# Chunked attention with a feed-forward: row-paired scores, a second batch by DMA transposes, a reordered front

## The chip, the cores and the metric

One NeuronCore of a Trainium2 chip. The metric is device time of one execution in microseconds (us); the kernel before takes 217.55 us (median of 3 runs, 217.46 to 218.55). Each profile is of one execution, and its span (first to last instruction) is some 1.7 us shorter than its time: 216.0 us for the kernel before. Times of different jobs differ a little (they ran on different chips), so every kernel below was timed in alternation with the kernel before, and the ratio of the two is what is compared.

## The reference, cut to what matters

```python
# 4 batches, 8 heads, 768 rows, head size 64, 8 memory rows; chunks of 32 rows,
# each sees 16 rows to the left, itself, 8 rows to the right and the memory
for c in range(S // 32):
    k_full = concat(mem_k, k[l_start:r_end]);  v_full = concat(mem_v, v[l_start:r_end])
    a = softmax(q[c] @ k_full.T / sqrt(64))
    out[c] = a @ v_full
x  = heads side by side                      # 4 x 768 x 512
xn = (x - mean) / sqrt(var + 1e-6) * g_ln
y  = x + max(xn @ w_ch1, 0) @ w_ch2          # 512 -> 2048 -> 512
```

The 3072 rows are 24 tiles of 128 rows; three tiles make a unit, two units a batch. Units and batches are counted from 0 here: what the recorded texts call the second unit is unit 1. "Up" and "down" are the two projections of a unit. The attention of a unit's three tiles runs among the projections of the unit before it.

## The kernel before: the parts that matter

Everything is scheduled by hand. A unit's program has 28 numbered steps: 16 column groups of the up projection, then 12 pieces of the down projection. `at(step, f)` puts other work into a step.

Scores take two heads at once on all 128 rows of TensorE. For this the queries lie in a buffer that is half zeros, `QZ`:

```python
def scores(b, t):                       # before
    for gg in range(2):
        for j in range(4):              # pair of heads
            nc.tensor.matmul(out=p[:, gg, 128 * j : 128 * j + 128],
                lhsT=KT[...128 rows, 128 columns], rhs=QZ[b % 2][:, g, j, :, :])   # 128 columns, half zeros
```

Keys and queries must be turned (head size onto the partitions). Batches 0 and 1 are turned on TensorE from a few large loads (four for batch 1, rows of 1 KB); batches 2 and 3 come as twelve token loads each (128 KB in rows of 128 B) and are turned by DMA transposes issued on SyncE ("crossbar"):

```python
def load_tokens(b, which, t): nc.gpsimd.dma_start(...)            # 128 tokens x 8 heads x 128 B
def cross_k(b, half, t0, t1): nc.sync.dma_start_transpose(KT, kraw)
def k_around(b, t0, t1):      4 x nc.gpsimd.tensor_copy(KT, KT)   # borders: a chunk's neighbours
def load_v_head(b, h):        nc.gpsimd.dma_start(V, v)           # values, batches 2 and 3
def v_around(b):              2 x nc.sync.dma_start(V, V)         # value borders
... cut ...
if u == 0: ... load_kq x4, load_v_group x6 for batch 1, inverse roots of tiles 0-2 at steps 19 to 21
if u == 1: kq_block(1, j, ...) at 5 and 11        # batch 1 turned on TensorE
           load_tokens(2, ...) x12 at 14
if u == 2: cross(2) at 0, 1; k_around at 8; load_v_head x8 at 8; second half of cross(2) at 14, 15
if u == 3: v_mem(2), v_around(2) at 1; k_around at 4
```

GpSimd issues the loads, SyncE the transposes, the output stores and the border copies; each works through its queue in order. GpSimd also computes each tile's inverse root, 1/sqrt(var + 1e-6), in that order.

The softmax here doesn't subtract the row's maximum and nothing guards it: scores larger than these inputs give would overflow.

## Time and profile before

| | kernel before |
|---|---|
| time, median (range) | 217.55 us (217.46 to 218.55) |
| span of the profile | 216.0 us |
| TensorE busy | 97% of the span |
| first up matmul (unit 0) | 18.27 us |
| unit 1 starts | 47.37 us |
| unit 2 starts | 74.65 us |
| unit 3 starts | 98.06 us |
| unit 4 starts | 121.39 us |

The unit starts are the starts of the first up matmul of each unit in the matmul timeline. In the line below the fields are packets, bytes, mean rate and how many packets were small:

```profile
DMA packets 87714, 27.37 MB, mean 127 GB/s; under 512 B 78297, under 2 KB 84185, under 8 KB 87642
```

### The profile page before, as it was taken

Reading aid. Unit: us, or ns where it says so; the run is one execution under the profiler, and the core shown is the slowest. Engines: PE = TensorE matmul, PEld = TensorE weight load, DVE = VectorE, ACT = ScalarE, POOL = GpSimd, SP = SyncE. Lnnn points to the kernel's source line nnn. Section 1 sums busy time; section 2 is a strip of 40 time slices with the busy share of each in tenths; the row PEclk is TensorE's granted clock in tenths of the full one; section 3 lists DMA queues with packets and bytes.
Section 4 is the critical chain, followed back from the end, with each engine's and each line's share of the span. In section 5 each row is a group of like instructions: output and inputs, shape, how many; then the busy total and the mean of one; then the engine's idle time right before and its main releaser. Section 6 shows DMA issues by size and latency. Waiting matters only on the chain.

```text
span 216.0 us, 5059 instructions
## 1 busy us (share of the span) xinstructions
PE 210.2 (97%) x2011; PEld 129.8 (60%) x2011; DVE 118.6 (55%) x274; ACT 99.7 (46%) x206; POOL 104.4 (48%) x185
## 2 busy tenths in 40 slices
PE   7999989999999999999999999999999999999993
PEld 2557866557765577546754676456754675466562
DVE  6967675685737548524375349224484447634222
ACT  4478437855893677302653167103761275314100
POOL 7993245699996318974004998507145000400000
PEclk9999999999999999999999999999999999999998
DMA  5999999999999989996312999997674101330012
GB/s 78 182 150 207 209 208 181 200 206 226 148 140 172 102 135 146 151 146 171 48 27 80 142 186 148 138 156 103 176 150 132 49 3 24 91 108 0 0 49 100
DMA packets 87714, 27.37 MB, mean 127 GB/s; under 512 B 78297, under 2 KB 84185, under 8 KB 87642
## 3 DMA queue, kind: packets, MB, share of 16 engines
q0 software_dynamic: 62128, 14.38, 78.2%
q1 hardware_dynamic: 25562, 12.66, 28.2%
q8 instruction: 16, 0.26, 0.5%
q14 instruction: 8, 0.07, 0.1%
HBM read 28.84 MB, written 6.29 MB: 163 GB/s over the span
## 4 chain that ended last, share of the span: by engine, by line
PE 94%; DVE 3%; ACT 1%; issue 1%; ACTq 0%
PE mm L377 37%; PE mm L394 37%; PE att L289 5%; PE att L309 3%; PE mm L366 3%; PE att L179 2%; PE mm L412 2%; PE mm L179 1%; DVE QZ L436 1%; ACT AT L296 1%; PE att L352 1%; PE att L366 1%; DVE rT L385 1%; PE mm L539 0%; DVE xn L329 0%
## 5 line engine op out<-in xcount | busy, mean ns | idle before, releaser
L377 PE MATMUL mm<-xT,w1c 128*128 128x384 f16 (+2 forms) x560 | 89.0, 313 | 0.6 <-DVE rT L385 0.6
L394 PE MATMUL mm<-w2c,rT 128*128 128x512 f16 x368 | 84.4, 379 | 0.0
L377 PEld LDWEIGHTS <-w1c 128*128 128x128 f16 x560 | 58.8, 114 | 23.6 <-issue 1.0
L383 ACT ACTIVATE rT<-mm 128x384 f16<-128x384 f32 (+2 forms) x74 | 33.1, 453 | 72.4 <-PE mm L377 50.2
L394 PEld LDWEIGHTS <-rT 128*128 128x128 f16 x368 | 34.7, 98 | 37.5
L385 DVE TENSOR_SCALAR rT<-mm 128x384 f16<-128x384 f32 (+2 forms) x66 | 34.9, 533 | 33.6 <-PE mm L377 33.5
L401 DVE SCALAR_TENSOR_TENSOR osb<-mm,rstd,xs 128x512 f32<-128x512 f32 x23 | 17.3, 750 | 41.8 <-PE mm L394 24.9
L296 ACT ACTIVATE AT<-att,band 104x512 f16<-104x512 f32 x48 | 30.2, 683 | 9.6 <-PE att L289 8.2
L338 POOL TENSOR_SCALAR veps<-squares 128x1 f32<-128x1 f32 x24 | 4.8, 200 | 42.7 <-ACT junk L335 41.3
L117 POOL DMA_DIRECT2D V<-in_v_dram x24 | 18.4, 772 | 11.0 <-DMA w1c<-in_moe_w_ch_dram 7.8
L335 ACT ACTIVATE junk<-xs,nmean 128x512 f16<-128x512 f32 x24 | 17.3, 721 | 7.1 <-DVE nmean L326 6.7
L329 DVE SCALAR_TENSOR_TENSOR xn<-xs,nmean,g_row 128x512 f16<-128x512 f32 x24 | 18.8, 782 | 0.9
L320 DVE SCALAR_TENSOR_TENSOR xs<-att,rec 128x512 f32<-128x512 f32 x24 | 16.6, 691 | 0.8
L289 PEld LDWEIGHTS <-KT 128*128 128x128 f16 x192 | 12.6, 98 | 4.6 <-issue 1.0
L277 POOL COPY QZ<-kraw 64x768 f16<-64x768 f16 x16 | 13.2, 826 | 3.9 <-DMA kraw<-qraw 3.4
L342 POOL TENSOR_TENSOR rstd<-veps,mhalf 128x1 f32<-128x1 f32 x24 | 13.7, 571 | 2.0
L289 PE MATMUL att<-QZ,KT 128*128 128x128 f16 x192 | 14.6, 219 | 0.0
L269 POOL COPY KT<-KT 128x128 f16<-128x128 f16 (+4 forms) x16 | 4.2, 292 | 18.2 <-DMA KT<-kraw 18.1
L123 POOL DMA_DIRECT2D V<-in_v_dram x16 | 12.0, 791 | 0.9 <-PE mm L377 0.7
L309 PEld LDWEIGHTS <-AT 104*64 104x64 f16 x384 | 7.5, 111 | 6.5 <-ACT AT L296 2.1
L242 POOL DMA_DIRECT2D qraw<-in_q_dram x12 | 11.3, 938 | 0.0
L242 POOL DMA_DIRECT2D kraw<-in_k_dram x12 | 11.2, 934 | 0.0
(76 smaller groups left out, 136.6 us busy)
## 6 DMA issues: line engine op xcount, KB each, us to landing
out_dram<-osb SPq DMA_DIRECT2D x23, 256.0 KB, 2.3
V<-in_v_dram POOLq DMA_DIRECT2D x36, 96.0 KB, 6.9
w1c<-in_moe_w_ch_dram POOLq DMA_DIRECT2D x4, 512.0 KB, 9.6
w2c<-in_moe_w_ch_dram POOLq DMA_DIRECT2D x4, 512.0 KB, 13.5
kraw<-in_k_dram POOLq DMA_DIRECT2D x12, 128.0 KB, 5.3
qraw<-in_q_dram POOLq DMA_DIRECT2D x12, 128.0 KB, 5.4
qraw<-in_q_dram POOLq DMA_DIRECT2D x3, 384.0 KB, 11.6
kraw<-in_k_dram POOLq DMA_DIRECT2D x3, 256.0 KB, 5.7
```

The lines of the kernel that those rows point to most:

```text
L117: nc.gpsimd.dma_start(out=V[b % 2][r : r + hi - lo, g, :, 0:64], in_=dram(v, b * H * HS + lo * D, [[64, hi - lo], [HS, H], [1, 64]]),)
L242: nc.gpsimd.dma_start(out=free(dst, 512 * t, [[64, H], [1, 64]]), in_=dram(src, b * H * HS + 128 * t * D, [[D, 128], [HS, H], [1, 64]]),)
L289: nc.tensor.matmul(out=p[:, gg, 128 * j : 128 * j + 128], lhsT=KT[b % 2][:, (4 * g + j) * KW : (4 * g + j) * KW + 128], rhs=QZ[b % 2][:, g ...
L296: nc.scalar.activation(out=free(a, 32 * c, [[512, 2], [64, 8], [1, 32]], KR), in_=free(p, 32 * c, [[512, 2], [64, 8], [1, 32]], KR), func= ...
L320: nc.vector.scalar_tensor_tensor(out=x.rearrange("p (h d) -> p h d", h=H), in0=free(p, 0, [[128, H], [1, 64]]), scalar=1.0, in1=free(r, 0, ...
L329: nc.vector.scalar_tensor_tensor(out=xn[i], in0=x, scalar=nmean[i], in1=g_row, op0=ALU.add, op1=ALU.mult,)
L335: nc.scalar.activation(out=junk, in_=xs[xi], func=ACTF.Square, bias=nmean[i], accum_out=squares[i],)
L377: nc.tensor.matmul(out=p, lhsT=free(w, i, [[4, 128]]), rhs=xT[u % 2][:, dt, lo:hi], start=(dt == 0), stop=(dt == 3),)
L383: nc.scalar.activation(out=o, in_=p, func=ACTF.Relu)
L385: nc.vector.tensor_scalar(out=o, in0=p, scalar1=0.0, scalar2=None, op0=ALU.max)
L394: nc.tensor.matmul(out=p, lhsT=rT[hc][:, 128 * i : 128 * i + 128], rhs=w2c[hc // 4][:, hc % 4, :], start=(hc == 0), stop=(hc == 15),)
L401: nc.vector.scalar_tensor_tensor(out=o, in0=p, scalar=rstd[t % 9], in1=xs[t % 9], op0=ALU.mult, op1=ALU.add,)
```

## The change

Its intent: scores of two heads run side by side, each on 64 of TensorE's rows, with dense queries, so that half of the streamed columns and all copies that spread queries into a zeroed buffer go; batch 1 is turned by the crossbar as batches 2 and 3 are, which takes 128 transposes off TensorE; and the front is reordered so that the first tile's work comes first, with batch 0's memory values copied on VectorE rather than by DMA.

```diff
-            nc.tensor.matmul(out=p[:, gg, 128*j : ...], lhsT=KT[b % 2][:, ...128],
-                             rhs=QZ[b % 2][:, g, j, :, :])
+            for par in range(2):
+                rows = slice(64 * par, 64 * par + 64)
+                nc.tensor.matmul(out=p[:, par, 64*(4*gg+j) : ...+64], lhsT=KT[b % 2][rows, ...128],
+                                 rhs=QT[b % 2][rows, ...64], tile_position=(64 * par, 0))
... cut: spread_q, clear_q and QZ go; keep_q copies once instead of twice ...
 # the front
-    v_mem(0)                               # memory rows of V by DMA
-    for g in range(6): load_v_group(0, g)
+    for g in range(3): load_v_group(0, g)  # the other three behind the band's arithmetic
+    keep_mem(0, 0, 6, vec)                 # memory rows of V on VectorE
+    # g_row: two one-row FP32 matmuls between the first and the second transposes
 ... cut: other filler counts between the pieces (stay_busy) ...
-    for hc in range(3): up(0, 1, hc, 0, True)     # first tile alone
+    for hc in range(2): up(0, 2, hc)              # two tiles
 # unit 0
-            for h in (0, 4):
-                for which in range(2): at(15, load_kq, 1, which, 0, 96, h, h + 4)
-            for g in range(6): at(23, load_v_group, 1, g)
+            for t in range(6):
+                for which in range(2): at(15, load_tokens, 1, which, t)
 # unit 1
-            kq_block(1, ...) at 5 and 11;  load_v_group(1, 6..11) at 0
+            cross(1) at 0 to 3;  k_around(1, 0, 4) at 8;  load_v_group(1, 0..1) at 8
+            k_around(1, 4, 6) at 13;  load_v_group(1, 2..11) at 13
 # units 2 and 3, for batch 2
-            cross(2) at 0, 1 and 14, 15;  k_around and load_v_head x8 at 8
+            cross(2) at 14, 15 and 17, 18;  k_around and load_v_head x8 at 22
-            v_mem, v_around at 1;  k_around at 4        (unit 3)
+            k_around at 2;  v_mem, v_around at 3        (unit 3)
```

Batch 1's loads and transposes now occupy GpSimd and SyncE during unit 1, and batch 2's transfers were moved back behind them. Fillers (`stay_busy`) are matmuls whose results nobody uses; they only keep TensorE busy.

## The prediction

> **What bounds the kernel now.** I read the page's busy shares first, then the chain that ended last, then the matmul, GpSimd and SyncE timelines, because one busy engine hides where the others will become the limit.
>
> ```profile
> PE 210.2 (97%) x2011; PEld 129.8 (60%) x2011; DVE 118.6 (55%) x274; ACT 99.7 (46%) x206; POOL 104.4 (48%) x185
> ...
> PEclk9999999999999999999999999999999999999998
> ...
> PE 94%; DVE 3%; ACT 1%; issue 1%; ACTq 0%
> ```
>
> TensorE is busy for 97% of the span at full clock and makes 94% of the chain. So a change pays only by matmul time taken out, or loses by a wait put in. The up and down projections (37% + 37% of the chain) are untouched. What the change can touch is read from the matmul timeline of the second half of the second unit (a unit is three 128-row tiles):
>
> ```profile
> 62.38 1.03 PE L394 MATMUL mm<-w2c,rT 128*128 128x512 f16 x4
> 63.24 0.61 PE L289 MATMUL att<-QZ,KT 128*128 128x128 f16 x8
> 63.69 1.89 PE L394 MATMUL mm<-w2c,rT 128*128 128x512 f16 x8
> 65.51 0.70 PE L309 MATMUL att<-V,AT 104*64 104x65 f16 x32
> 66.14 1.90 PE L394 MATMUL mm<-w2c,rT 128*128 128x512 f16 x8
> ...
> 70.58 0.44 PE L309 MATMUL att<-V,AT 104*64 104x65 f16 x16
> 70.96 2.76 PE L394 MATMUL mm<-w2c,rT 128*128 128x512 f16 x12
> ```
>
> Starts count here, not durations, because matmuls overlap. One scores call (8 matmuls) takes 63.69 - 63.24 = 0.45 us, 56 ns each. A down matmul takes 0.216 us (63.24 - 62.38, over 4). The values, which use half of the array's columns each, are already run in pairs: 32 take 65.51 to 66.14 = 0.63 us, 16 take 70.58 to 70.96 = 0.38 us, so 8 pairs cost 0.25 us and about 0.12 us is fixed. Ahead of them there is another 0.09 us (63.69 + 8 x 0.216 = 65.42, but the start is 65.51). Thus one excursion into the split array costs about 0.21 us besides its 31 ns per pair.
>
> **What the Trainium skill says.** "TensorEngine Tiling (Array Packing)", section Key Properties: changing the tiling mode drains TensorE. The 0.09 + 0.12 us agree. "TensorE: Matmul & The Clock Gate", Part 3: matmuls on different row groups run at once. The trace of before has only column pairs, whose 31 ns agree; no row pair has run yet. The same page, section on the 16 sub-arrays: ScalarE and VectorE are strict FIFO and GpSimd is FIFO per core. The GpSimd timeline below agrees: nothing passes a waiting issue. "DMA: Bandwidth & Descriptors", Specifications: at least 512 B per transfer for line rate. The trace agrees: 202 GB/s in the weight-loading stretch from 14 to 48 us, but 12 loads of 128 KB with 128 B rows land 0.86 us apart, some 150 GB/s.
>
> **Part by part.**
>
> Scores. A call becomes 16 matmuls of 64 columns on 64 rows, in 8 pairs. If a row pair costs the 31 ns of a column pair, that is 8 x 31 = 0.25 us, plus 0.21 us for going in and out of the mode: 0.46 against 0.45 us. Over 24 calls this is nothing (+0.2 us). Halving the streamed columns is eaten by the mode switch. What the dense form does save is off TensorE: the two half-height copies of each query block become one, the GpSimd spreading copies (13.2 us) disappear, and the VectorE clearing of the padded queries (four of 1.34 us) goes.
>
> Those clears did hurt once:
>
> ```profile
> 27.51 1.34 DVE QZ L436
> 29.31 1.46 PE mm L377 x8
> ```
>
> The matmul timeline has 0.55 us of idle there, put down to VectorE, about 0.7 us counted from start to start. In exchange VectorE gets a 48x64-element copy of memory values and small memsets in the same steps, so I credit 0.5 us.
>
> Batch 1 by crossbar. Two blocks of 64 transposes go:
>
> ```profile
> 51.43 1.48 PE att L179 x64
> 52.91 4.02 PE mm L377 x24
> 56.94 1.48 PE att L179 x64
> ```
>
> 2 x (1.48 + 0.09 of entry) = 3.1 us of TensorE, the only large certain saving.
>
> Front. The memory-value rows no longer come by a DMA of 120 KB on eight partitions. In before that transfer shared the engines from 9 to 13 us, where the rate falls to 120 GB/s with the load queue getting 60 to 100. The four value loads after it ended 4.9 us after the second one, where 0.65 us each would be 2.6. Every later weight should therefore land about 2 us earlier. First scores came at 12.35 us behind VectorE's clears and key copies. Without the clears I work out about 11.6. But the first projection now waits for two tiles rather than one: its start stays near 18.5, and the first four column groups of two tiles end at about 20.8 instead of 21.1. With the clear this makes about 1.0 to 1.2 us at the end of the first up phase.
>
> Raw sum: 3.1 + 1.2 - 0.2 = 4.1 us. Now what takes it back.
>
> The order on GpSimd. The four loads of batch 1 keys and queries become twelve, and they stand ahead of the inverse roots of tiles 0 to 2. Before:
>
> ```profile
> 38.89 0.67 POOL L107 DMA_DIRECT2D qraw<-in_q_dram  x1 [1.73 <-DMA w2c<-in_moe_w_ch_dram]
> 39.64 0.19 POOL L338 TENSOR_SCALAR veps<-squares 128x1 f32<-128x1 f32 x1
> 39.91 1.06 POOL L342 TENSOR_TENSOR rstd<-veps,mhalf 128x1 f32<-128x1 f32 x1
> ```
>
> Each issue waits for the landing of the one eight earlier (here the third w2 chunk). Twelve issues of 0.93 us, the last behind the fourth token load's landing: w2's last chunk landed at 42.2, less 2.3 is about 40; four tokens at 0.86 give 43.7; the last issue ends near 44.7. Three roots follow at 0.9 to 1.3 us each: about 46.2, 47.1 and 48.0. The first output add of unit 0, which ran at 45.7 in before, now waits for the root until 46.2, and the three tiles' down results hold three of the four accumulators. So the second unit's up phase starts when VectorE has passed the third output add, near 49.1. I get its fifth column group at 49.9 us; in before it stood at 47.37 + 4 x 0.65 = 50.0. The whole 1.2 us gained so far is spent in this wait.
>
> The crossbar for batch 1. On SyncE the transposes stand behind the third output and the memory-value transfer, which itself waits for GpSimd's clearing of the second value buffer (after the roots): about 50 us. In before:
>
> ```profile
> 76.32 3.79 SPq L248 DMA_TRANSPOSE KT<-kraw  x2
> 80.28 2.57 SPq L254 DMA_TRANSPOSE kraw<-qraw  x2
> ```
>
> 6.5 us passed from this start to the first value load behind the key borders (82.8). From about 50 to 51.3 this puts the first two value loads at 57 to 58 and the other ten, behind the second border copy, at 61.3 to 63. They land three us after issue. Values of batch 1's second tile, reached by TensorE near 64.2, then find their rows at 64.5 to 67: a new wait of 0 to 2.8 us. The author moved these steps one later, so I take 1.0.
>
> Sum: 4.1 - 1.1 - 1.0 = 2.0 us off: 217.55 - 2.0 = 215.5 us.
>
> **Rivals.** First, row pairs do not overlap, or weight loads of 128 columns serialise, at 56 ns per pair: 0.66 us a call, 24 x 0.2 = 4.8 us lost, in all about 219 to 220. For it: the array has never been used so here. Against it: column pairs overlap well, and weight loads in before are hidden under 56 ns. Second, the row mode costs no drain: then 0.2 us per call is gained, 3 us after unit 1, in all about 212.5. Against it: both switches of the column mode cost. Third, GpSimd and the crossbar are as late as my worst case: 2.8 us of wait eat the 3.1, and the time stays at 217.5. For it: each link is in the old trace, and they are in series. Fourth, no wait appears, since DMA lands sooner: all 4.1 us are kept, 213.4. For it: the schedule looks tuned to trace.
>
> **Range and chances.** Middle 215.5; the third and fourth rival span 213.4 to 217.5, and the less likely first two widen it to 212.5 to 218.5. Faster by over 2% means below 213.2, which needs all gains with no new wait, or a drain-free row mode: 0.16. Slower by over 2% is above 221.9, which needs failed overlap and the late crossbar: 0.04. Within 2%: 0.80.
>
> **What would show it.** Score calls: start to start 0.44 to 0.48 us with a gap of about 0.1 us on either side; 0.25 would show no drain, 0.66 no overlap. No transposes of batch 1 on TensorE. On GpSimd the first root near 46 us instead of 40, and a TensorE gap of about 1 us around 47 waiting for an output add. Later a gap before the values of batch 1's second tile, its release being a value load. First scores at 11 to 12 us; the last w2 chunk landing near 40. I am wrong if the roots are on time, if unit 2's up phase starts before 71.5 or after 75 us (74.65 before), or if anything after unit 2 moves by over 0.5 us beyond the score calls themselves.

## More of the kernel before

TensorE's waits in the kernel before, from the view of waits (line waited on, releaser, us in total, times, longest). The first of them is in the start-up. There is almost nothing else to wait for:

```profile
PE mm L366 <- DVE counts L460: 1.2, 1, 1.2
PE mm L377 <- DVE rT L385: 0.6, 1, 0.6
PE att L309 <- ACT AT L296: 0.3, 1, 0.3
```

## The result, and the profile after

The changed kernel takes 237.0 us (median of 4 runs, 234.83 to 238.91), ratio 1.0848 with a 95% interval of 1.0763 to 1.0933: slower by 8.5%, far outside the predicted range. A ratio here is the mean time of one kernel's fast runs over that of the other's in the same rounds, so it is not quite the ratio of the medians quoted. Executions over 1.5% slower than the fastest of the same kernel are left out of the means. The profiled run of this first job was slow, so the kernel was run again (`after_again`, in three rounds: 235.54 us, 234.92 to 236.75, ratio 1.0825, interval 1.0772 to 1.0878). All lines of the changed kernel below are from that fast profile, span 233.3 us.

From the page: TensorE's busy share, its granted clock in 40 slices, the chain that ended last, and the packets.

```profile
PE 214.9 (92%) x2050; PEld 124.5 (53%) x2050; DVE 108.3 (46%) x257; ACT 88.9 (38%) x183; POOL 101.1 (43%) x185
...
PEclk9859999999998899999995999999999999999999
...
DMA packets 104890, 28.82 MB, mean 124 GB/s; under 512 B 97105, under 2 KB 101361, under 8 KB 104818
...
PE 51%; DMA 7%; issue 2%; POOL 2%; SPq 1%; ACT 1%; DVE 0%; POOLq 0%
```

Three things are to be seen. TensorE is no longer all of the chain: DMA, GpSimd and SyncE have come in. (This chain is followed back only to 82.85 us, so its shares add to some 64%.) The clock line, a row of nines before, has dips at slices 2 and 3 (6 to 17 us), 13 and 14 (70 to 82 us) and 22 (122 to 128 us), and each holds a half-speed stretch. And 17,176 packets more move only 1.45 MB more: they are small.

The starts of the units tell where the 17.3 us of span went:

| | before | after | the stretch that ends here is longer by |
|---|---|---|---|
| unit 0 starts | 18.27 | 22.30 | 4.0 (the front) |
| unit 1 starts | 47.37 | 50.73 | -0.7 |
| unit 2 starts | 74.65 | 83.37 | 5.4 |
| unit 3 starts | 98.06 | 106.76 | 0.0 |
| unit 4 starts | 121.39 | 138.99 | 8.9 |
| end of span | 216.0 | 233.3 | -0.3 |

So there are three places, and they have different causes.

**The front.** Here are the two kernels in stretches (us from the start; length, then busy time of each engine, then the granted clock, DMA share and GB/s). First the kernel before, then the changed one:

```profile
6.00:10.00 4.00, 4.00 (x105) 2.30 (x104) 3.69 (x15) 1.51 (x4) 3.96 (x11) 1.00 1.68 182
10.00:14.00 4.00, 4.00 (x57) 2.12 (x55) 3.36 (x8) 3.27 (x9) 3.69 (x9) 1.00 3.23 127
```

```profile
6.00:10.00 4.00, 3.63 (x89) 2.39 (x89) 3.00 (x7) 0.86 (x2) 3.80 (x12) 0.94 1.58 161
10.00:14.00 4.00, 4.00 (x62) 1.96 (x56) 1.82 (x5) 1.20 (x3) 4.00 (x7) 0.50 1.61 105
```

TensorE is "busy" for all of 10 to 14 us in both, but at a clock of 1.00 before and 0.50 after. The busy share hides this; the clock column shows it.

**Unit 1.** TensorE's waits in the changed kernel:

```profile
PE att L307 <- DMA V<-V: 6.7, 1, 6.7
PE att L307 <- DMA V<-in_v_dram: 3.6, 3, 2.5
PE mm L375 <- ACT xT L355: 1.6, 2, 0.8
PE att L287 <- DMA QT<-qraw: 1.6, 2, 1.1
```

And its matmul timeline of unit 1 (start, length, instruction, in brackets the idle time before it and what ended it):

```profile
50.73 10.64 PE L375 MATMUL mm<-xT,w1c 128*128 128x384 f16 x64 [0.84 <-ACT xT L355]
...
64.97 0.29 PE L287 MATMUL att<-QT,KT 64*128 64x64 f16 x8 [1.10 <-DMA QT<-qraw]
...
66.16 0.41 PE L287 MATMUL att<-QT,KT 64*128 64x64 f16 x16
66.50 1.90 PE L392 MATMUL mm<-w2c,rT 128*128 128x512 f16 x8
...
72.69 0.19 PE L307 MATMUL att<-V,AT 104*64 104x65 f16 x1 [2.53 <-DMA V<-in_v_dram]
73.73 0.42 PE L307 MATMUL att<-V,AT 104*64 104x65 f16 x15 [0.85 <-DMA V<-in_v_dram]
74.08 0.41 PE L287 MATMUL att<-QT,KT 64*128 64x64 f16 x16
74.42 3.54 PE L392 MATMUL mm<-w2c,rT 128*128 128x512 f16 x8
```

The transposes are gone (3.1 us saved), but the scores wait for the crossbar's queries, the values for the value rows, and then eight down matmuls take 3.54 us where eight took 1.89 us before: from 74.4 to 77.8 us the clock is at half speed (the clock column gives 0.68, 0.50, 0.50 and 0.61 for the four stretches of 1 us from 74 us on). The waits of 2.53 + 0.85 us thus cost 1.65 us more: they are paid about one and a half times.

The link that the prediction had put first is there too. GpSimd's timeline of the changed kernel shows the fourth of twelve token loads, which waited for a w2 chunk to land as the same place did before, then the last, then the first inverse root:

```profile
41.02 0.88 POOL L247 DMA_DIRECT2D qraw<-in_q_dram  x1 [2.02 <-DMA w2c<-in_moe_w_ch_dram]
...
48.18 0.92 POOL L247 DMA_DIRECT2D qraw<-in_q_dram  x1
49.17 0.19 POOL L336 TENSOR_SCALAR veps<-squares 128x1 f32<-128x1 f32 x1
49.45 0.57 POOL L340 TENSOR_TENSOR rstd<-veps,mhalf 128x1 f32<-128x1 f32 x1
```

**Unit 3.** The changed kernel's chain, in order of time, shows how batch 2 came late. Each line is a link: start, length, what.

```profile
98.63 3.31 DMA KT<-kraw
...
107.21 2.20 POOL V L122 x3
109.41 8.76 DMA V<-in_v_dram
...
119.03 5.17 DMA V<-V
...
124.33 1.09 PE att L307 x32
```

The key transposes land, GpSimd copies the key borders, issues eight value loads behind them, these land 8.76 us later, only then do the value border copies start, and they take 5.17 us. In the kernel before SyncE issued the same border copies 18 us sooner:

```profile
100.57 0.60 SPq L131 DMA_DIRECT2D V<-V  x1
101.22 1.53 SPq L132 DMA_DIRECT2D V<-V  x1
```

**What came as predicted.** In the matmul timeline above a score call starts at 66.16 us and the down matmuls go on at 66.50: 0.34 us, with 0.10 us of entry before it 0.44 us, where it was 0.45. The row pairs do overlap, and what the call spends on entering and leaving the mode eats the gain.

### The profile page after: what moved, and what is told of

Its sections match the earlier page's. It is cut to its first block, busy times and chain, and to the rows that moved or that the text cites. A ratio compares the mean times of both kernels' runs of the same rounds, so it can differ in the third digit from the quotient of the medians.

```text
span 237.2 us, 5099 instructions
## 1 busy us (share of the span) xinstructions
PE 217.2 (92%) x2050; PEld 125.2 (53%) x2050; DVE 108.3 (46%) x257; ACT 88.8 (37%) x183; POOL 100.8 (42%) x185
## 4 chain that ended last, share of the span: by engine, by line
PE 50%; DMA 8%; issue 2%; POOL 2%; SPq 1%; ACT 1%; DVE 0%; POOLq 0%
PE mm L375 23%; PE mm L392 21%; DMA V<-in_v_dram 4%; PE att L307 2%; DMA V<-V 2%; PE att L287 2%; PE mm L410 1%; DMA KT<-kraw 1%; POOL V L122 1%; POOL KT L274 0%; ACT junk L333 0%; SPq L130 0%; SPq L344 0%; ACT xT L355 0%; DVE osb L415 0%
## 5 line engine op out<-in xcount | busy, mean ns | idle before, releaser
L375 PE MATMUL mm<-xT,w1c 128*128 128x384 f16 (+2 forms) x528 | 90.6, 327 | 4.3 <-ACT xT L355 4.3
L392 PE MATMUL mm<-w2c,rT 128*128 128x512 f16 x368 | 87.4, 389 | 0.0
L381 ACT ACTIVATE rT<-mm 128x384 f16<-128x384 f32 (+2 forms) x66 | 31.8, 482 | 87.3 <-PE mm L375 65.9
L399 DVE SCALAR_TENSOR_TENSOR osb<-mm,rstd,xs 128x512 f32<-128x512 f32 x23 | 17.3, 750 | 50.4 <-PE mm L392 38.1
L294 ACT ACTIVATE AT<-att,band 104x512 f16<-104x512 f32 x48 | 30.2, 684 | 18.3 <-PE att L287 16.3
L333 ACT ACTIVATE junk<-xs,nmean 128x512 f16<-128x512 f32 x24 | 17.3, 722 | 12.0 <-DVE nmean L324 6.9
L307 PE MATMUL att<-V,AT 104*64 104x65 f16 x384 | 10.9, 205 | 11.2 <-DMA V<-V 7.7
L274 POOL COPY KT<-KT 128x128 f16<-128x128 f16 (+4 forms) x24 | 6.5, 299 | 28.9 <-DMA KT<-kraw 28.9
L307 PEld LDWEIGHTS <-AT 104*64 104x64 f16 x384 | 8.6, 118 | 19.0 <-issue 15.2
L247 POOL DMA_DIRECT2D kraw<-in_k_dram x18 | 16.8, 936 | 1.3 <-DMA w2c<-in_moe_w_ch_dram 1.2
L247 POOL DMA_DIRECT2D qraw<-in_q_dram x18 | 16.9, 937 | 1.0 <-DMA w2c<-in_moe_w_ch_dram 1.0
L317 DVE RECIPROCAL rec<-att 128x8 f32<-128x8 f32 x24 | 4.9, 204 | 24.1 <-PE att L307 19.8
L287 PEld LDWEIGHTS <-KT 64*128 64x128 f16 x384 | 7.5, 99 | 8.5 <-issue 8.4
```

Source lines behind the costliest of these rows:

```text
L247: nc.gpsimd.dma_start(out=free(dst, 512 * t, [[64, H], [1, 64]]), in_=dram(src, b * H * HS + 128 * t * D, [[D, 128], [HS, H], [1, 64]]),)
L294: nc.scalar.activation(out=free(a, 32 * c, [[512, 2], [64, 8], [1, 32]], KR), in_=free(p, 32 * c, [[512, 2], [64, 8], [1, 32]], KR), func= ...
L307: nc.tensor.matmul(out=p[64 * gg : 64 * gg + 64, h // 4, c0 : c0 + 65], lhsT=AT[t % 3][0:KR, h % 2, 4 * gg + h // 2, :], rhs=V[b % 2][0:KR ...
L333: nc.scalar.activation(out=junk, in_=xs[xi], func=ACTF.Square, bias=nmean[i], accum_out=squares[i],)
L375: nc.tensor.matmul(out=p, lhsT=free(w, i, [[4, 128]]), rhs=xT[u % 2][:, dt, lo:hi], start=(dt == 0), stop=(dt == 3),)
L381: nc.scalar.activation(out=o, in_=p, func=ACTF.Relu)
```

## The experiments

Seventeen runs followed. In the diffs `-` is the changed kernel and `+` the experiment unless it is said otherwise.

### Three parts taken apart

`rows_alone`: the kernel before with the dense queries and row-paired scores only.

```diff
 # kernel before, with scores(), keep_q(), QT of the changed kernel; QZ, clear_q, spread_q gone
```

> Only the dense queries and the row-paired scores; front, batch 1 on TensorE and the loads as in the kernel before. Theory (the slowdown comes from the order of loads and from waits, not from the new scores): a call is 0.34 us plus 0.09 us of entry against 0.45, so 24 calls give back 0.5 us, and the VectorE clears that cost 0.7 us are gone: 216.0 to 217.0 us, ratio 0.993 to 0.998. Rival (row mode itself costs, by switching or by starving ScalarE or the clock): above 219 us, ratio over 1.007.

Measured: 216.45 us (216.23 to 216.85), ratio 0.9943 (0.9906 to 0.9981). As expected: a small gain, so the scores are not the loss. In its profile unit 0 is 0.7 us shorter than before (28.36 against 29.10 us), which fits VectorE's clears; units 1 to 6 are as long as before to 0.1 us.

`new_front_rows`: the changed kernel, batch 1 turned on TensorE again and batch 2's schedule of before. So it is `rows_alone` plus the new front.

```diff
-            for t in range(6): ... at(15, load_tokens, 1, which, t)
+            for h in (0, 4): ... at(15, load_kq, 1, which, 0, 96, h, h + 4)
-            cross(1) ..., k_around(1) ...
+            kq_block(1, j, 0, NG, "att") at 5 and 11
```

> The changed kernel with batch 1 turned on TensorE again and batch 2's schedule as before: what is left is scores and front. Theory (the new front loses 2.0 us by the end of the first unit and nothing after it): 219 to 220 us, ratio 1.006 to 1.011, TensorE at half clock for some us around 10 to 15 us, first up matmul near 21.9 us. Rival (the front starts the later waits as well, because its weights land later): 224 us or more.

Measured: 219.2 us (218.72 to 219.37), ratio 1.0063 (1.0018 to 1.0108). The front costs 219.2 - 216.45 = 2.75 us. What is left to the changed kernel, 235.54 - 219.2 = 16.3 us, is batch 1's crossbar with the schedules that were moved for it.

`after_again`, the changed kernel itself beside these:

> The changed kernel once more, for a profile in its fast state and as the mark for the runs beside it. 235 to 238 us, 8 to 9% over the kernel before, with three long TensorE waits at the same places as in the first profile: about 3.6 us before the second unit's up phase, about 4 us before the values of batch 1's second tile, about 7.8 us before the values of batch 2's first tile. If the first profile was a one-off of its slow state, one of these is missing or half as long here.

Measured as told above, 235.54 us. By its own test the expectation fails in part: two of the three waits are there in a fast run (3.4 us for the values, 6.7 us in unit 3), but the one before unit 1 is 0.84 us, not 3.6, so that one was of the slow profile.

### The front's clock

`warm_front`: `new_front_rows` with the two one-row FP32 matmuls moved behind the last transposes, and six filler matmuls of 512 columns in their place rather than one.

```diff
-    for i in range(2): nc.tensor.matmul(out=banks[i][:, 256:512], lhsT=ones32, rhs=g_one[...])
-    stay_busy(1, spare)
+    stay_busy(6, spare)
 ... second transposes ...
+    for i in range(2): nc.tensor.matmul(out=banks[i][:, 256:512], lhsT=ones32, rhs=g_one[...])
```

> Beside the run of new front and row scores without the batch 1 crossbar (219.2 us): the two one-row float matmuls that spread the gain vector go behind the last query transposes, and six filler matmuls stand in their place; same work otherwise, even more filler. Theory (the front loses because too little counts as TensorE activity between 6 and 10 us, so the clock halves until about 15 us and the fillers themselves hold up the transposes): clock stays full, scores start near 12.5 instead of 13.7 us, first up matmul near 20.2 instead of 21.7, time 217.3 to 218.2 us, ratio 0.998 to 1.003. Rival (the front loses by the later loads and by waiting for two tiles): clock as it may, the time stays at 219 us.

Measured: 217.97 us (217.65 to 219.31), ratio 1.0013 (0.9967 to 1.0058). The same stretch as above, first in `new_front_rows`, then in `warm_front`:

```profile
10.00:14.00 4.00, 4.00 (x52) 1.73 (x50) 2.07 (x5) 0.87 (x2) 4.00 (x7) 0.50 1.61 107
```

```profile
10.00:14.00 4.00, 4.00 (x76) 2.19 (x74) 1.61 (x4) 1.36 (x4) 4.00 (x6) 1.00 1.51 100
```

The clock is 1.00, and 219.2 - 217.97 = 1.2 of the 2.75 us come back (1.1 by the ratios, whose intervals overlap; in the profiles the first up matmul starts 1.5 us sooner, at 20.21 instead of 21.72 us). The other 1.5 us stay: 20.21 us is still later than the 18.26 of `rows_alone`, and TensorE is never idle for more than 0.43 us on the way. The new front puts more stages and fillers in a row, but in this profile the first weights also landed only at 19.97 us (17.85 in `new_front_rows`, 18.21 in `rows_alone`), so the matmul could hardly have come sooner. The two were not taken apart.

### Batch 2's chain in unit 3

`heads_early`: batch 2's eight value loads at step 2 of unit 2, ahead of the key border copies.

```diff
-                for h in range(H): at(22, load_v_head, 2, h)
+                for h in range(H): at(2, load_v_head, 2, h)
```

> The changed kernel with batch 2's eight value-head loads issued at step 2 of the third unit instead of step 22; nothing else. Theory (the 7.8 us wait is the chain of keys' crossbar, border copies, value heads, value borders, all on GpSimd and SyncE in program order): the wait before batch 2's first values goes, with the half clock after it, so 226 to 228.5 us, ratio 1.04 to 1.05. Rival (the DMA engines are full there, so that loads issued sooner only delay the crossbar): 232 us or more.

Measured: 230.04 us (229.23 to 231.83), ratio 1.0577 (1.0514 to 1.0639). Between the two: 2.4 us of wait on the border copies were left, since these stood on SyncE behind four crossbar pairs and three stores.

`borders_early`: the border copies moved as well.

```diff
-                at(3, v_mem, 2); at(3, v_around, 2)          # unit 3
+                at(13, v_mem, 2); at(13, v_around, 2)        # unit 2, ahead of cross(2)
```

> The changed kernel with batch 2's value heads at step 2 of the third unit and also the memory rows and the two border copies at step 13, ahead of the crossbar transposes in SyncE's order. With the heads alone 2.4 us of wait were left, put down to the border copies, which stood behind four transposes and three outputs. Theory (they are late by program order, not by the time of the copy): the wait before batch 2's first values is gone, 226.5 to 228 us, ratio 1.040 to 1.047. Rival (the copies take their 5 us wherever they stand, or push the key crossbar out): still 230 us.

Measured: 227.19 us (226.26 to 228.31), ratio 1.0426 (1.0372 to 1.0481). No wait for the border copies is left, and unit 3 takes 23.36 us again (32.23 in the changed kernel, 23.33 before). So 235.5 - 227.2 = 8.3 us of the loss (8.7 by the ratios), half of it, is this chain: not batch 1's transfers but where batch 2's were moved to make room.

### Unit 1: which load is it?

`roots_first`: the inverse roots ahead of six of the twelve token loads on GpSimd.

```diff
-                at(15, load_tokens, 1, which, t)
+                at(15 if t < 3 else 22, load_tokens, 1, which, t)    # roots are at 19 to 21
```

> The changed kernel with six of the twelve token loads of batch 1 and the clearing of the second value buffer swapped on GpSimd, so that the three roots stand behind six loads rather than twelve. Theory (roots behind token issues hold the output adds, then the accumulators, then the memory rows and the crossbar): the wait before the second unit goes (1.0 us, and the slow restart), and the crossbar starts 2 to 4 us sooner, so the wait for values shrinks as well: 230 to 233 us, ratio 1.057 to 1.07. Rival (the crossbar is bound by the tokens' landing, which the swap puts later): 235 us or more.

Measured: 237.54 us (234.93 to 238.89, one run of four slow), ratio 1.0859 (1.0782 to 1.0936). The rival is right. The first root ran at 42.70 us and unit 1 started at 49.28 rather than 50.73, but the scores then waited 3.5 us for key borders: the later tokens landed later.

`old_front`: the changed kernel with the front of before.

```diff
 # clear_v, the loads and the order of the first tiles as in the kernel before, with keep_q's single copy
```

> The changed kernel with the front of the kernel before (dense queries kept), so with the batch 1 crossbar and all later orders as changed. Theory (front and crossbar add up: the front's 2.7 us are between the two runs without the crossbar, 219.2 and 216.45): 232 to 234 us, ratio 1.065 to 1.075. Rival (the later waits hang on DMA landings, which both fronts share, so an earlier front only waits longer): 235 us or more.

Measured: 236.69 us (233.71 to 239.33), ratio 1.077 (1.0695 to 1.0845). Two of the four runs were slow; the two fast ones took 235.75 and 233.71 us. The interval reaches into the theory's ratios and also takes in the changed kernel's 1.0825, so this run does not decide. Its profile is of a slow run (waits of 3.0 us before unit 1 and of 9.3 us on the value borders), so no cause is read from it.

`values_first`: six of batch 1's value groups at the start of unit 1, ahead of the key borders.

```diff
-            at(8, k_around, 1, 0, 4); V groups 0-1 at 8; V groups 2-11 at 13
+            V groups 0-5 at 0; at(8, k_around, 1, 0, 4); at(13, k_around, 1, 4, 6); V groups 6-11 at 13
```

> The changed kernel, but batch 1's first six value groups load at the start of the second unit, ahead of the key border copies, and the other six behind the second border copy. My theory: what TensorE waits for in the second half of the second unit is the landing of value rows that stand behind the border copies in GpSimd's queue; with six groups ahead of them the 3 to 4 us of wait for the values and the half-clock restart behind it go, and the time falls by 4 to 5.5 us against the changed kernel, to 230 to 231.5 us, ratio 1.057 to 1.063. Rival: GpSimd is the bound itself, so the six issues only push the border copies back and the scores wait in place of the values: 234 us or more.

Measured: 237.73 us (237.1 to 238.15), ratio 1.091. The rival's verdict, though not quite its cause: the wait for values went, and in its place the scores waited 6.4 us for the crossbar's queries. On SyncE the first two pairs took 5.52 and 4.22 us (4.83 and 2.62 in the changed kernel), with six value groups landing beside them.

`roots_first` and `values_first` each moved the wait to another transfer, which is what a shared resource looks like. The candidates were two: a bad order, or simply too much for the DMA engines.

### Order or amount?

`best2`: a version meant to win. Front of before, row-paired scores, batch 1 by crossbar, roots ahead of the tokens, value groups 0 to 5 at the end of unit 0, batch 2's schedule of before.

```diff
 # against the changed kernel, besides the old front
-                at(19 + t, root, t, t)
+                at(9 + 2 * t, root, t, t)             # ahead of the tokens at 15
-            at(23, clear_v, 1, nc.gpsimd)
+    clear_v(1, nc.gpsimd)                              # before unit 0
+            for g in range(6): at(26, load_v_group, 1, g)              # unit 0
-            at(8, k_around, 1, 0, 4); V groups 0-1 at 8; at(13, k_around, 1, 4, 6); V groups 2-11 at 13
+            at(8, k_around, 1, 0, 4); V groups 6-11 at 8; at(13, k_around, 1, 4, 6)
```

> A version meant to beat both: before's front, the row-paired scores and dense queries, batch 1 by crossbar, but with the inverse roots of the first three tiles ahead of the token loads, the second value buffer cleared before unit 0, six value groups loaded at the end of unit 0 and the rest behind the first border copy, and batch 2's schedule of before. My theory, the waits and not the crossbar cost the time: the 3.1 us of transposes are kept, 213 to 214 us, ratio 0.98. Rival: GpSimd's and the DMA queues' order still does not let the crossbar's inputs land in time, and a wait of 3 us or more comes back with its clock restart: 216.5 us or more.

Measured: 223.87 us (223.44 to 224.73), ratio 1.0283. A miss: TensorE waits 8.1 us for the crossbar's queries. SyncE's timeline shows why; the line is the first pair of key transposes:

```profile
48.91 8.28 SPq L253 DMA_TRANSPOSE KT<-kraw  x2
```

`values_behind`: `best2` with those six value groups behind the first key borders.

```diff
 # against best2
-            for g in range(6): at(26, load_v_group, 1, g)              # unit 0
+            V groups 0-5 at 8, behind k_around(1, 0, 4); V groups 6-11 at 13   # unit 1
```

> The version meant to beat both (run best2, 223.87 us), with one edit: batch 1's first six value groups are loaded behind the first key border copies instead of at the end of unit 0, so they no longer travel beside the crossbar's first transposes. My theory: the transposes share the DMA engines with whatever else lands. In best2 the first pair of key transposes held SyncE for 8.28 us while six value groups and the last tokens landed; without the values it should take some 4 us, as the first pair of batch 2 does in the kernel before (3.79), the wait of TensorE before the scores should fall from 7.8 us to about 2 to 3.5, and the time to 218 to 220 us; the first values may then wait a little themselves. Rival: the transposes are slow because of the tokens' own landing or by themselves, and the pair stays over 7 us: 223 us or more.

Measured: 223.8 us (221.25 to 224.66), ratio 1.0215. Of the expectation one part holds: the wait before the scores fell from 8.1 to 1.4 us. The pair still took 6.43 us, because the last tokens were landing beside it, and the time did not follow: only the profiled run, 221.25 us, is clearly below those of `best2`. (The ratios of `best2` to `best5`, 1.0215 to 1.0283, have intervals that overlap; among these five the waits can be told apart, the times cannot.)

`best3`: `values_behind` with the token loads in the order in which the crossbar needs them, and the first transposes started inside unit 0.

```diff
 # against values_behind
-            k0, q0, k1, q1, ... k5, q5 at 15;  cross(1) at 0, 1 and 2, 3 of unit 1
+            k0..k3, q0..q2, k4, k5, q3..q5 at 15;  cross(1) at 25, 26 of unit 0 and 10, 11 of unit 1
-            k_around(1, 0, 4) and V groups 0-5 at 8 of unit 1
+            k_around(1, 0, 4) and V groups 0-5 at 2 of unit 1
```

> As values_behind, but the token loads come in the order in which the crossbar needs them (seven for its first four transposes, then five), and these transposes are issued inside unit 0's last steps, between its output stores, so that they start near 46 us rather than 49; value groups behind the first border copies at the start of the second unit, the second four transposes and their borders from step 10. My theory: with the transposes 3 us earlier and no values beside them the inputs of batch 1's first scores (about 59.5 us) land by 57, nothing waits for over 0.5 us, and the 3.1 us of TensorE transposes become a gain: 213 to 214.5 us, ratio 0.98. Rival: there is too much for the DMA engines to carry between 40 and 65 us (tokens, transposes, values, output), and a wait of over 1.5 us with its clock restart remains: 216 us or more.

Measured: 223.59 us (221.98 to 223.93), ratio 1.0228. The pair took 5.75 us; 2.6 us of wait for queries, 1.2 for values, and 2.5 for projection inputs that stood behind batch 2's crossbar. The rival again.

`best4`: only the seven token loads that the first four transposes read go ahead of them; the other five come behind six value groups.

```diff
 # against best3
-            twelve load_tokens(1) at 15 of unit 0
+            k0..k3, q0..q2 at 15 of unit 0;  k4, k5, q3..q5 at 3 of unit 1, behind V groups 0-5
-            second half of cross(1) at 10, 11;  V groups 6-11 and k_around(1, 4, 6) at 13
+            V groups 6-11 at 4;  second half of cross(1) at 14, 15;  k_around(1, 4, 6) at 15
 ... cut: batch 2's twelve token loads in the order of need ...
```

> As best3 (223.59 us), with the second unit's transfers in the order of need: only the seven token loads that the first four crossbar transposes read stand ahead of them; then the first six value groups; then the other five token loads, the other value groups, and the second four transposes (which wait for those tokens); batch 2's tokens in the order of need as well. My theory, that what costs is transfers of a later need landing beside the transposes: the first key pair takes 4 us or less on SyncE (5.75 in best3), TensorE waits in the second unit for less than 1 us in all (4.2 us in best3), the third unit's up phase starts at 71 to 72.5 us (75.88), and the time is 213.5 to 216 us. Rival, that the tokens, transposes and values of a whole batch are more than this unit can carry in any order: over 2 us of waits remain and the time stays over 218 us.

Measured: 224.05 us (223.26 to 225.9), ratio 1.0271. The total misses, and yet this run settles most. SyncE's first key pair:

```profile
46.13 3.02 SPq L253 DMA_TRANSPOSE KT<-kraw  x2
```

It takes 3.02 us instead of 8.28, with only the last tokens' tail beside it. Unit 1 has no wait at all and lasts from 46.47 to 70.44 us, 23.97 us; it was 27.28 us before. So in unit 1 the crossbar does save the predicted 3.1 us (3.3 here). But what had been deferred came up later, in the view of waits:

```profile
PE att L307 <- DMA V<-V: 5.5, 1, 5.5
PE att L287 <- DMA QT<-qraw: 2.7, 2, 2.3
```

`best5` moved those two loads ahead in their turn (batch 1's last tokens after four value groups, batch 2's value loads before its key borders, its border copies before its second crossbar set).

```diff
 # against best4
-            V groups 0-5 at 2, five tokens at 3, V groups 6-11 at 4             # unit 1
+            V groups 0-3 at 2, five tokens at 3, V groups 4-11 at 4
-            k_around at 8; load_v_head x8 at 8; cross(2) at 14, 15; v_around at 1 of unit 3
+            load_v_head x8 at 2; k_around at 8; v_around at 14; cross(2) at 14, 15
```

> best4's profile showed no wait of TensorE in the second unit (it lasted 23.97 us, 27.28 in the kernel before), but the deferred loads then held up unit 2 (2.7 us before the scores of batch 1's fourth tile, on the second crossbar set) and unit 3 (5.5 us on batch 2's value borders, half clock behind each). best5 takes best4 and moves these two: after four value groups rather than six come batch 1's last five token loads, and batch 2's value heads are loaded ahead of its key borders, with the value border copies on SyncE ahead of the second crossbar set. My theory, order of need throughout: no wait of over 0.5 us is left, the third unit starts by 71 us and the time is 213 to 215 us, below both kernels. Rival, the amount: the loads pushed back come up once more as a wait of over 2 us in unit 2 or 3, and the time stays over 217.5 us.

Measured: 222.85 us (221.47 to 223.44), ratio 1.022. The rival: 3.3 us of wait for the projection inputs, which stand behind batch 2's crossbar on SyncE, 2.3 for queries.

`best6`: `best4`, with slack instead of haste. Batch 1's second half is attended seven steps later in unit 2; batch 2's crossbar stands behind the unit's own projection inputs.

```diff
 # against best4, unit 2
-                attend(((2, 7, 7, 7), (4, 7, 8, 8), (9, 13, 13, 13)))
+                attend(((9, 14, 14, 14), (11, 14, 15, 15), (16, 20, 20, 20)))
-                cross(2) at 0, 1 and 14, 15;  load_v_head at 8;  v_around at 1 of unit 3
+                load_v_head at 2;  cross(2) at 21, 22;  v_around at 23;  cross(2) at 24, 25
```

> best4's second unit (no wait there, 23.97 us instead of 27.28 in the kernel before), with the two places mended where the deferred loads came up later: the attention of batch 1's second half runs five to seven steps later in unit 2 (the steps that units 3 and 5 use), so that its keys and queries have landed; and batch 2's value heads are loaded ahead of its key borders, its crossbar sets and value border copies stand on SyncE behind this unit's own projection inputs, the border copies between the two sets. My theory, order of need alone: unit 2 starts near 70.5 us, no wait of over 0.5 us is left after it, and the rest lasts about 141 us as in the kernel before (216.0 - 74.65 = 141.35): some 211.5 us of span, 212.5 to 214.5 us of time, ratio 0.98. Rival, the amount: some load is late again by over 2 us and the time stays over 217 us.

Measured: 219.42 us (218.48 to 221.34), ratio 1.0108 (1.0051 to 1.0164). Short of the aim; 4.9 us of waits left, all on batch 2.

`best7`: `best6` with batch 2's first key tokens and crossbar moved into the stretch in which SyncE had been idle.

```diff
 # against best6
-            at(15, k_around, 1, 4, 6); twelve load_tokens(2) at 15               # unit 1
+            k0..k3 of batch 2 at 15; at(15, k_around, 1, 4, 6); the other eight at 15
-                cross(2) at 21, 22; k_around at 23                               # unit 2
+                cross(2) at 3, 4; k_around at 10
```

> best6 came to 219.42 us; its profile has no wait before 93.6 us (third unit's start 70.45, 74.65 in the kernel before), and then 4.9 us of waits on batch 2: projection inputs 1.1, second queries 1.5, value border copies 2.3. SyncE stood idle there from 74.2 to 83.9 us, and GpSimd from 67.4 to 72.7 us, waiting for batch 1's last border copies with batch 2's token loads behind it. best7 loads batch 2's first four key tokens ahead of that wait and issues batch 2's first crossbar set into SyncE's idle stretch. My theory, order alone: the 4.9 us go but for at most 1, 212 to 214.5 us, ratio 0.975 to 0.985, below both kernels. Rival, the amount: the transposes beside the token loads are slow and batch 1's fourth tile or batch 2 waits again, over 216.5 us.

Measured: 224.71 us (224.22 to 226.06), ratio 1.0291 (one run of the kernel before beside it took 436.6 us). A clear miss. SyncE's pair, and the DMA view of 68 to 78 us (issues: how many, KB each, median us from issue to landing):

```profile
82.33 5.83 SPq L253 DMA_TRANSPOSE KT<-kraw  x2
```

```profile
kraw<-in_k_dram POOLq DMA_DIRECT2D x4, 128.0 KB, 10.9
```

SyncE was idle, but the DMA engines were not: the four key loads took 10.9 us to land beside batch 1's last transposes (5.3 us in `values_behind` from 44 to 46 us, where nothing but tokens travelled), the crossbar came late, and 8.3 us of wait followed for the projection inputs, whose transposes stood behind it on SyncE. An idle queue is not an idle resource.

`best8`: `best6` again, and no transfer moved; TensorE only asks for batch 2's tiles later, and for one of batch 1's a step sooner.

```diff
 # against best6
+            elif u == 2: attend(((9, 14, 14, 14), (11, 14, 15, 15), (15, 19, 19, 19)))
+            elif u == 3: attend(((12, 18, 18, 18), (13, 18, 19, 19), (18, 21, 21, 21)))
```

> best7 put batch 2's crossbar beside its own token loads and lost (224.71 us): the four key tokens then landed 8 to 12 us after their issue and the transposes took 5.8 us a pair. best8 goes back to best6 (219.42 us) and moves no transfer at all: in unit 3 the first two tiles' scores wait three and two steps longer and their values four (the third tile two and one), in unit 2 the third tile comes one step earlier, so that TensorE has projection work where best6 left it 4.9 us of waits. My theory: those waits shrink to at most 1.5 us, 214 to 216.5 us, ratio 0.983 to 0.995. Rival: with less slack behind them the projection inputs of unit 4 come late in place of it, or the run-to-run spread of the transfers (best6 218.48 to 221.34) hides it: over 217.5 us.

Measured: 216.81 us (215.92 to 218.73), ratio 0.9937 (0.9907 to 0.9966): faster than the kernel before by 0.6% (the interval leaves out 1) and than the changed kernel by a long way. Its waits after the front, in a profile that caught the slowest of its seven runs (218.73 us):

```profile
PE att L307 <- DMA V<-V: 1.3, 2, 1.0
...
PE att L287 <- DVE xs L318: 0.8, 1, 0.8
PE mm L375 <- DMA xT<-xn: 0.8, 1, 0.8
...
PE att L287 <- DMA QT<-qraw: 0.3, 1, 0.3
```

In that profile unit 1 is 3.2 us shorter than in `rows_alone` (23.98 against 27.19 us), while units 2, 3 and 5 are 1.1, 3.9 and 0.4 us longer, the 3.2 us of waits included. The median run is 1.9 us shorter than the profiled one, so gain and loss about cancel: `rows_alone`, which has no crossbar for batch 1, has the same ratio (0.9943). So the 16.3 us were order and slack, not amount: the same transfers, placed well and asked for later, cost nothing net. But in eight tries they did not pay either. Whether the 3.2 us of unit 1 can be kept stays open; both best versions beat the two kernels by 0.6% and by some 8%.

## Why the prediction was wrong, point by point

**Bound by TensorE, scores neutral, transposes worth 3.1 us: right.** A call took 0.44 us (0.46 foreseen), the rows part gained 1.2 us in all (some 0.3 foreseen, the clears' 0.5 less 0.2), and `best4`'s unit 1 was 3.3 us shorter than before. The first two rivals, row pairs that do not overlap and a switch without drain, are both out.

**The front: wrong in sign.** The step was "Every later weight should therefore land about 2 us earlier", taken from a stretch of slow DMA before that was laid to the memory rows. In the changed front the last three value loads stand behind the band's arithmetic on GpSimd, and the first weights are asked for at 11.65 us (10.83 before). They landed at 18.93 us (17.82 before, 17.85 in `new_front_rows`), the last w2 chunk at 43.56 (42.22 before, near 40 foreseen): later, not earlier. And the prediction worked with TensorE's starts as if its clock were given: it never asked whether the new mix of transposes, one-row FP32 matmuls and few fillers would hold it. It did not (0.50), and the first scores came at 14.30 us, not at 11 to 12. The 1.2 us foreseen held 0.5 for VectorE's clears, which `rows_alone` has without the new front; in place of some 0.7 us gained the front cost 2.75, about 1.2 of it the clock. The Trainium skill could have warned: "TensorE: Matmul & The Clock Gate", Part 4: PE-mode transpose, says that transpose-mode work does not count as busy for the clock in the same way, and the kernel's transposes run in that mode. The trace agrees as far as `warm_front` tells: six fillers instead of one before the second transposes, with the one-row matmuls moved behind these, brought the clock from 0.50 to 1.00; it does not separate the two, and the kernel before, with as many transposes, stayed at 1.00.

**GpSimd's order: right in kind.** First root foreseen at 46 us, found at 49.17; a TensorE gap of about 1 us foreseen, 0.84 found. The 3 us are the front's error carried on: the fourth token load waited for the third w2 chunk, which landed at 40.72 us (38.60 before, and the prediction took 2 us off that), and eight more issues of about 0.9 us followed. Moving the roots ahead (`roots_first`) did not shorten the whole.

**Batch 1's crossbar: the right wait, mis-sized.** The step was "The author moved these steps one later, so I take 1.0". The waits of unit 1 came to 6.0 us: 1.6 for queries and 3.6 for values, plus 0.8 before unit 2 for the last tile's inputs. They were mis-sized for three reasons. The crossbar, foreseen at about 50 to 51.3 us, started at 55.30: behind the late roots stood the clearing of the second value buffer and the memory-value transfer (53.76 us). From there 7.87 us passed to the first value load, not 6.5, and 14.3 to the other ten, not some 11.5: the durations were taken from stretches of the old trace in which transposes and loads ran with other company, and with more beside them they stretch further (3.02 us a pair nearly alone, 5.75 to 8.28 beside token and value loads). Only the landing of those ten, 3.1 to 3.8 us after their issue, came as foreseen. And a wait is not paid once: unit 1 became 5.4 us longer although 3.1 us of work had gone, so 8.5 us were lost, of which 6.0 are waits. Of the other 2.5 us, 1.65 are the matmuls at half clock in the 3.54 us line; the rest was not taken apart.

**"If anything after unit 2 moves by over 0.5 us": this was the largest miss.** The prediction worked out no cost for the lines of the diff that move batch 2's crossbar and value loads back, and held that nothing after unit 2 would change. Unit 3 became 8.9 us longer, and `borders_early`, in which unit 3 is back to 23.36 us, shows that this chain is the cause (8.3 us of the whole time): crossbar, borders, eight value loads behind them, 8.76 us of landing, 5.17 us of border copies. A link of each kind stands in the old trace, so the sum could have been tried as it was for batch 1.

**The chances.** 0.04 for slower rested on two named ways to fail. The way that happened, many serial links each a little late, with half-clock stretches after the waits, was not among the rivals. The range was also narrower than its own rivals: the first, 215.5 + 4.8, gives 220.3 us, and the range stops at 218.5.

## What to carry to other kernels

When a change moves work from a busy engine to DMA, sum every chain that its diff moves, for the batches after it too, and take the durations beside the transfers they will run with, not alone; the same transfers cost 16 us in one order and nothing net in another in which TensorE also asked for them later. Give a late transfer slack by asking for its data later before you hurry its issue: an idle queue (SyncE, GpSimd) does not mean that the DMA engines behind it are idle. Count a TensorE wait of some 3 us about one and a half times, because here the clock was at half speed for some 3.4 us after it, and read the clock column beside the busy share.

## What the Trainium skill lacked or had wrong

- "TensorE: Matmul & The Clock Gate", Part 4: its remark that transpose-mode work does not count as busy for the clock stands where one reads about transposes, not with the clock in Part 1; and whether one-row FP32 matmuls count is not said. Here a front of transposes, two such matmuls and one to three fillers between them fell to a clock of 0.50 from 10 to 14 us; with six fillers instead of one before the second transposes, and the two matmuls moved behind these, it held 1.00.
- The same page, Part 1, describes waits of more than one window of about 3.4 us. Here two waits, 2.53 and 0.85 us, neither of them that long and with one matmul of 0.19 us between, were enough (3.57 us together, so the sum fits the page's figure): the next eight matmuls of 512 columns took 3.54 us instead of 1.89.
- "TensorEngine Tiling (Array Packing)", Key Properties, says that a change of mode drains TensorE, but not for how long: here about 0.10 us going in (row pairs) and 0.12 us coming out (from the column pairs before), so that 8 row pairs of 64 columns cost 0.44 us and nothing is gained over 8 full matmuls of 128 columns (0.45 us).
- "Advanced Engine Details and Errata", X-Bar Transpose (TRN2), calls transpose DMAs as fast as regular ones and gives a bandwidth for them. No number is given there or elsewhere for transposes beside small loads: a pair of 256 KB each held SyncE for 3.02 us nearly alone (2.65 at 98.63 us in the changed kernel), 5.75 beside token loads and 8.28 beside token and value loads, and token loads of 128 KB landed after 10.9 us rather than 5.3.
- "DMA: Bandwidth & Descriptors" has a ceiling for transfers from SBUF to SBUF but no duration for small ones between partitions such as the value borders (a copy of 220 KB and one of half of that): 5.17 us from the issue of the second to landing.
